# Second-layer V loads between the K loads, three half tiles of K loaded a second time, and softmax denominators on GpSimd, in a two-layer decode kernel

## The chip, the cores and the metric

The kernel runs on one core of a Trainium2 chip. The metric is the device time of one execution in microseconds (us), and the figure compared is the median over several runs. The engines are named as the profile names them: PE is TensorE (PEld its weight loads), DVE is VectorE, ACT is ScalarE, POOL is GpSimd, SP is SyncE, whose queue issues the loads.

## The reference

Four sequences (B = 4) each decode one token with D = 512 channels. Two layers are applied, each an attention block and then a gated feed-forward block, both behind a layer norm and added to the residual. Both layers use **the same weights and the same K and V caches**:

```python
x = x + _A_ref(_layernorm(x), k_cache, v_cache, wq, wo)
x = x + _B_ref(_layernorm(x), w_gate, w_up, w_down)
x = x + _A_ref(_layernorm(x), k_cache, v_cache, wq, wo)   # layer 2: same caches, same weights
x = x + _B_ref(_layernorm(x), w_gate, w_up, w_down)
```

`_A_ref` projects x to 32 query heads of 128; there are 8 groups of K and V, each shared by 4 heads, with 4096 positions: scores, softmax over the positions, weighted sum of V, projection with `wo`. `_B_ref` is sigmoid(x wg) * (x wu), times wd, with F = 1792. All inputs are bfloat16. One group of K or of V of one batch element is 1 MB, so one batch element has 8 MB of K and 8 MB of V.

## The kernel before, in words

**Tiles.** A group of K or V is moved in two half tiles (q = 0, 1) of 128 x 2048 bfloat16, 512 KB each. They go into a ring of 22 slots in SBUF (`ring`, `NS = 22`); all weights have places of their own. In what follows a "load" is one half tile, a "batch" is one of the 4 sequences, written b, and l = 0, 1 is the layer.

**Stages of a batch.** For l = 0 the 16 loads of K are transposed in place by DVE (`transpose_k`, L475), in 32-bit units. `spread` makes a block form of the queries (`q_spread`, a matmul to `M_ps` and a DVE multiply into `qbd`, L466). `scores` (L488) multiplies the queries by the transposed K into one of three PSUM banks `S_ps`, for two halves s of four groups. `softmax` takes the maximum (DVE, L504 to L523), the exponentials with their sums `ls` (ACT, L528), transposes the result on PE through `PT_ps` (L536, L547 copy it out) into `pt_sb`, and makes the inverse denominators `winv`: a DVE product of `ls` and a selector into `dsel` (L553), two fp32 matmuls with ones into `M_ps`, a reciprocal (L559). `values` (L573) multiplies the V loads by `pt_sb` into `O_ps`; a DVE multiply by `winv` takes the result out (L582). `y_proj` applies `wo`. `cross` then does everything from there to the next layer's input: residual, layer norm, wg, wu, the gate, wd, residual, layer norm; `q_proj` makes the queries of layer 1. Matmuls built by the helper `mm` all have line L298.

**Two layers, one load of K.** K of batch b stays in its 16 slots, transposed, until the scores of layer 1 have been made from it; it is loaded once. V is loaded once for each layer: for layer 0 while layer 0's output is formed, and again for layer 1, for which the softmax of layer 1 must be done first.

**Order of the loads.** SP issues all loads in the order in which they are written in the program: wq and K of batch 0, four groups of V, wo, wg, four groups of V, wu, wd; then for b = 1, 2, 3

```python
for g in range(pre):            # pre = 0
    load_v(1, b - 1, g)
load_k(b, 0)
load_k(b, 1)
for g in range(8):
    load_v(0, b, g)
for g in range(pre, 8):
    load_v(1, b - 1, g)
```

and at the end V of batch 3 for layer 1. A load waits until the slot that it gets is free; every load behind it waits too.

**Order of the other work.** A planner (`_Sched.place`) fixes it before the kernel is built. Each piece of work has an engine, an assumed duration and a priority (lower goes first); the planner steps through time and gives every engine a fixed order, and every load a slot, the one that falls free first by its own reckoning. Loads are reckoned at `RATE` GB/us on one shared bus, with constants for the start and the landing. On the chip each engine runs its list strictly in that order and waits at semaphores, so a piece that waits holds up all pieces behind it on its engine. The priorities before are `PX, PS, PV, PC, PK = 0, 2, 2.2, 4, 2.1`: the way through `cross` and `q_proj` first, then layer 1's scores (1), layer 0's (2), the transposes of K (2.1), the V products (2.2).

Of the kernel before, what the change touches and what calls it, by code (L numbers as in the profile page):

```python
# [11 lines left out]
LAT = 0.2  # L12
RATE = 0.409


class _Op:
    __slots__ = (
        "eng", "fns", "dur", "prio", "sem", "inc", "deps", "after", "left", "users", "est", "start", "end", "seq",
        "needed", "value", "tile", "bytes", "lab",
    )  # L20
# [14 lines left out]
class _Sched:  # L35
# [6 lines left out]

    def put(self, eng, fns, dur, prio, reads=(), writes=(), dma=None, tiles=(), uses=(), nbytes=0):
        op = _Op()
        op.eng, op.dur, op.prio, op.bytes = eng, dur, prio, nbytes
        op.fns = list(fns) if isinstance(fns, (list, tuple)) else [fns]
        op.sem, op.inc, op.needed = dma or eng, 16 if dma else 1, dma is not None
        op.value = op.tile = op.start = op.end = None
        op.deps, op.after, op.users = [], [], []
        op.lab = ",".join(list(writes) + [dma or ""])  # L50
        for k in list(reads) + list(writes):
            w = self.last_write.get(k)
            if w is not None:
                self._dep(op, w, eng == "pe" and w.eng == "pe")
        for k in writes:
            for r in self.readers.get(k, ()):
                self._dep(op, r, r.eng == eng and r.sem == eng)
        for t in tiles:
            self._dep(op, t.load, False)
        for t in list(tiles) + list(uses):  # L60
            t.ops.append(op)
        for k in writes:
            self.last_write[k] = op
            self.readers[k] = []
        for k in reads:
            if k not in writes:
                self.readers.setdefault(k, []).append(op)
        op.seq = len(self.all)
        self.all.append(op)
        return op  # L70
# [5 lines left out]
    def load(self, tile, fn, nbytes):  # L76
        op = self.put("sp", fn, 0.55, 0, dma="slot", nbytes=nbytes)
        op.tile = tile
        tile.load = op
        return op  # L80

    def place(self):
# [15 lines left out]
        held = {}  # L98
        spi = 0

        def slot_time(s):
# [16 lines left out]
        while True:  # L118
# [27 lines left out]
            if o.eng == "sp":  # L146
# [11 lines left out]
                if o.bytes:  # L158
                    b0 = max(free_at["bus"], t + o.dur + 1.0)
                    free_at["bus"] = b0 + o.bytes / (RATE * 1e6)  # L160
                    self.bus.append((b0, free_at["bus"], o))
                    finish(o, free_at["bus"] + 1.2)
                else:
                    finish(o, t + 2.5)
            else:
                pending[o.eng].remove(o)
                free_at[o.eng] = t + o.dur
                finish(o, t + o.dur if o.sem == o.eng else t + 2.5)
        left = [o for o in self.all if o.end is None]
# [28 lines left out]
def bass_interleave_layers__gqa_block_cached__glu_gated_glu__decode_kernel(nc, A_x, A_k, A_v, A_wq, A_wo, B_x, B_wg, B_wu, B_wd, out):  # L198
# [67 lines left out]
    winv = [sb(f"winv{i}", [P, 16]) for i in range(4)]  # L266
    dsel = sb("dsel", [P, 2, 16])

# [37 lines left out]
    S.put("sp", lambda e: e.dma_start(x16[0:16, :], A_x.rearrange("b o (k p) -> (b o k) p", k=KD)), 0.55, 0, writes=["x16"], dma="x")  # L306
    S.put("pool", lambda e: e.memset(ident_b[:], 0.0), 0.15, 0, writes=["ident_b"])
    S.put("pool", affine(ident_b, ident_b[:], [[-1, P]], 0, 1.0), 0.3, 0, reads=["ident_b"], writes=["ident_b"])
    for key, ap, v in (("neg", neg, -1.0 / D), ("pos", pos, 1.0 / D), ("mhalf", mhalf, -0.5), ("ones", ones, 1.0)):
        S.put("dve", lambda e, ap=ap, v=v: e.memset(ap, v), 0.08, 0, writes=[key])  # L310
    for name, t in (("mask_a", mask_a), ("sel_den", sel_den)):
        S.put("pool", lambda e, t=t: e.memset(t[:], 0.0), 0.15, 0, writes=[name])
    for g in range(4):
        m = mask_a[32 * g:32 * g + 32, g * R:(g + 1) * R]
        S.put("pool", lambda e, m=m: e.memset(m, 1.0), 0.1, 0, reads=["mask_a"], writes=["mask_a", "sel_den"])
        v = sel_den[:].rearrange("p (g h) -> p g h", g=4)[:, g, :]
        for a in range(4):
            S.put("pool", affine(sel_den, v, [[-1, R]], -(32 * g + 4 * a), 1.0), 0.2, 0, reads=["sel_den"], writes=["sel_den"])
    for name, t, v in (("ml0", ml, 1.0), ("mt", mt, 0.0), ("S0", S_ps[0], 0.0), ("S1", S_ps[1], 0.0), ("S2", S_ps[2], 0.0)):
# [4 lines left out]
    vt = {}  # L324
    K, V = {}, {}

    def load_piece(src, q):
# [8 lines left out]

    def load_k(b, s):
        for q in range(2):
            for g in range(4 * s, 4 * s + 4):
                K[b, g, q] = load_piece(A_k[b, g], q)  # L340

# [4 lines left out]
    def load_w(key, o, i, nbytes):  # L346
        S.put("sp", lambda e: e.dma_start(o, i), 0.55, 0, writes=[key], dma=key, nbytes=nbytes)  # L347

# [28 lines left out]
    load_wd()  # L377
    pre = 0
    for b in range(1, B):
        for g in range(pre):  # L380
            load_v(1, b - 1, g)
        load_k(b, 0)
        load_k(b, 1)
        for g in range(8):
            load_v(0, b, g)
        for g in range(pre, 8):
            load_v(1, b - 1, g)
    for g in range(8):
# [41 lines left out]
    def rstd(mult, rs, rs_key, nb, prio):  # L430
# [6 lines left out]
            "pool", lambda e: e.tensor_tensor(rs, vpe[:, 0:nb], mhalf[:, 0:nb], ALU.pow), 0.6, prio,  # L437
            reads=["vpe", "mhalf"], writes=[rs_key],
        )

    def q_proj(s, xT_of, n, dst, dkey, prio, xkey):
# [9 lines left out]
        S.put("act", lambda e: e.activation(dst, M_ps[:, 0:16 * n], ACTF.Copy), 0.25, prio, reads=["M"], writes=[dkey])  # L451

    cnt = {"u": 0, "o": 0, "pt": 0}

# [14 lines left out]

    def transpose_k(b, g, q, prio):  # L470
        t = K[b, g, q]

        def fn(e):
            v = ring[t.slot].bitcast(dt.int32)
            return e.transpose(v, v)  # L475
        S.put("dve", fn, 1.2, prio, writes=[f"kT{b}{g}{q}"], tiles=[t])

    def scores(b, s, u, prio):
        for q in range(2):
            fns = []  # L480
            bank, bkey = S_ps[(2 * u + q) % 3], f"S{(2 * u + q) % 3}"
            for nn in range(NQ):
                for gi in range(4):
                    t = K[b, 4 * s + gi, q]

# [7 lines left out]
            S.put(  # L493
                "pe", fns, 1.85, prio, reads=[f"qbd{u % NQB}"] + [f"kT{b}{4 * s + gi}{q}" for gi in range(4)],
                writes=[bkey], uses=[K[b, 4 * s + gi, q] for gi in range(4)],
            )

    def softmax(u, rs, rs_key, prio):
# [41 lines left out]
        for t4 in range(4):  # L540
# [8 lines left out]
        )  # L549
        i0 = ls.unsqueeze(2).broadcast_to([P, 2, 16])  # L550
        i1 = sel_den[:].unsqueeze(1).broadcast_to([P, 2, 16])
        S.put(
            "dve", lambda e: e.tensor_tensor(dsel[:], i0, i1, ALU.mult), 0.2, prio + 1,  # L553
            reads=["ls0", "ls1", "sel_den"], writes=["dsel"],
        )
        fns = [mm(M_ps[:, 480:496], col(ones), dsel[:, q, :], q == 0, q == 1) for q in range(2)]
        S.put("pe", fns, 0.7, prio + 1, reads=["dsel", "ones"], writes=["M"])
        S.put(
            "dve", lambda e: e.reciprocal(winv[pi][:], M_ps[:, 480:496]), 0.18, prio + 1, reads=["M"],  # L559
            writes=[f"winv{pi}"],  # L560
# [3 lines left out]
    def values(l, b, s, pi, prio, gis=range(4)):  # L564
        if not len(gis):
            return
        for gi in gis:
# [13 lines left out]
        S.put(  # L581
            "dve", lambda e: e.tensor_tensor(o, O_ps[:, c0:c1], winv[pi][:, c0:c1], ALU.mult), 0.2, prio - 1.5,  # L582
            reads=["O", f"winv{pi}"], writes=[f"oT{l}{s}{gi}" for gi in gis],
# [102 lines left out]

    PX, PS, PV, PC, PK = 0, 2, 2.2, 4, 2.1

# [9 lines left out]
    def attend(l, b, s, prio, u=None):  # L698
        if u is None:
            u = spread(l, b, s, prio)  # L700
        if l == 0:
            for q in range(2):
                for gi in range(4):
                    transpose_k(b, 4 * s + gi, q, PK)
        scores(b, s, u, prio)
        return softmax(u, rs_q[l][:, b:b + 1], "rs_q0" if l == 0 else f"rs_q1{b}", prio)
# [10 lines left out]
    for s in range(NH):  # L717
# [13 lines left out]
        )  # L731
        pis[0, 0, s] = attend(0, 0, s, PS)
    for b in range(B):
        if b > 0:
            values(1, b - 1, 0, pis[1, b - 1, 0], PV, range(pre))
        for s in range(NH):
            for gis in (range(0, 3), range(3, 4)):
                values(0, b, s, pis[0, b, s], PV, gis)
                y_proj(0, s, PX, gis)
        if b > 0:  # L740
            values(1, b - 1, 0, pis[1, b - 1, 0], PV, range(pre, 4))
        cross(0, b, PX)
# [4 lines left out]
        if b < B - 1:  # L747
            us += [spread(0, b + 1, s, PS) for s in range(NH)]
        if b > 0:
            values(1, b - 1, 1, pis[1, b - 1, 1], PV)  # L750
        for s in range(NH):
            pis[1, b, s] = attend(1, b, s, 1, us[s])
        if b < B - 1:
            for s in range(NH):
                pis[0, b + 1, s] = attend(0, b + 1, s, PS, us[NH + s])
    for s in range(NH):
        for gis in (range(0, 3), range(3, 4)):
            values(1, B - 1, s, pis[1, B - 1, s], PV, gis)
            y_proj(1, s, PX, gis)
# [42 lines left out]
```

## Time and profile before

| what | value |
|---|---|
| median of 5 runs | 343.33 us (341.32 to 344.94) |
| the profiled execution: its time, and its span (first to last instruction) | 344.94 us, 342.6 us |
| outside the span in that execution | 2.3 us |
| bytes loaded | 115.32 MB, mean 337 GB/s over the span |
| busy: PE, PEld, DVE, ACT, POOL | 219.7, 170.2, 138.6, 52.6, 10.5 us |
| granted TensorE clock, mean | 0.605 |
| loads: V, K, weights | 128 and 64 of 512 KB; 4 wq and 4 wo of 1 MB; wg, wu, wd of 1.75 MB |

The page's slices show the share of busy time over the span; the row of GB/s shows what the 16 DMA engines moved in each slice. "A <- B" in the table of groups and of waits means that A sat idle until B released it. SPq is the queue that issues the loads.

### The profile page before, as it was taken

What the parts mean: (1) busy time and instruction counts of PE and PEld (TensorE: products, weight loads), DVE (VectorE), ACT (ScalarE), POOL (GpSimd) and SP (SyncE); (2) the same over time, 40 slices, a digit from 0 to 9 for tenths busy, and PEclk for the clock granted to TensorE, in tenths of its full rate; (3) what the DMA queues carried; (4) which work ended last, traced back from release to release, by engine and by line L of the source; (5) the groups of instructions that cost most, each with busy time, mean ns of one, the idle gap of its engine ahead of it and who ended that gap; (6) DMA issues with size and microseconds to landing.
All of it is one profiled execution on the core that took longest, in us unless ns stands there. A gap on an engine that the chain in (4) does not pass through costs nothing.

```text
span 342.6 us, 11870 instructions
## 1 busy us (share of the span) xinstructions
PE 219.7 (64%) x5426; PEld 170.2 (50%) x5426; DVE 138.6 (40%) x338; ACT 52.6 (15%) x128; POOL 10.5 (3%) x38
## 2 busy tenths in 40 slices
PE   1332861264678694878843896789546968796666
PEld 1202551154634283776521485784324758765566
DVE  3777620000859820101599730015998300143011
ACT  1003030000023330000322130002312300014000
POOL 6000000000000000000000000000000000000001
PEclk9999965555565555555855555557655555578555
DMA  7999999999559979978899999979999999989910
GB/s 264 379 397 408 409 349 366 409 404 374 204 158 397 401 239 411 383 276 309 267 407 408 371 353 362 371 273 322 388 412 408 378 326 416 318 291 367 409 77 2
DMA packets 36897, 115.32 MB, mean 337 GB/s; under 512 B 3312, under 2 KB 9200, under 8 KB 36848
## 3 DMA queue, kind: packets, MB, share of 16 engines
q1 hardware_dynamic: 36816, 114.57, 89.3%
q8 instruction: 42, 0.69, 0.8%
q14 instruction: 7, 0.06, 0.0%
q10 hardware_dynamic: 32, 0.00, 0.0%
HBM read 114.56 MB, written 0.00 MB: 334 GB/s over the span
## 4 chain that ended last, share of the span: by engine, by line
DMA 42%; PE 29%; DVE 14%; SPq 7%; issue 6%; ACT 1%; DVEq 0%; ACTq 0%
DMA ring<-in_A_v_cache_dram 30%; DMA ring<-in_A_k_cache_dram 10%; PE O_ps L573 7%; PE S_ps L488 6%; PE Y_ps L298 6%; DVE ring L475 6%; SPq L331 5%; PE M_ps L298 4%; PE G_ps L298 3%; DMA wo<-in_A_wo_dram 3%; DVE ml L504 3%; SPq L347 2%; PE PT_ps L298 1%; ACT p_sb L528 1%; DVE qbd L466 1%
## 5 line engine op out<-in xcount | busy, mean ns | idle before, releaser
L573 PE MATMUL O_ps<-pt_sb,ring 128*128 128x4 bf16 x2048 | 67.5, 166 | 41.4 <-DMA ring<-in_A_v_cache_dram 30.3
L573 PEld LDWEIGHTS O_ps<-pt_sb,ring 128*128 128x128 bf16 x2048 | 62.8, 104 | 49.8 <-issue 24.3
L475 DVE STREAM_TRANSPOSE ring<-ring 128x1024 int32<-128x1024 int32 x64 | 76.7, 1223 | 14.8 <-DMA ring<-in_A_k_cache_dram 14.6
L488 PE MATMUL S_ps<-ring,qbd 128*16 128x512 bf16 x512 | 53.3, 567 | 13.1 <-DVE ring L475 13.1
L528 ACT ACTIVATE p_sb<-S_ps,cols 128x512 bf16<-128x512 f32 x32 | 24.6, 772 | 85.5 <-DVE cols L523 85.5
L582 DVE TENSOR_TENSOR oT<-O_ps,winv 128x12 bf16<-128x12 f32 (+2 forms) x26 | 4.5, 174 | 79.0 <-PE O_ps L573 78.9
L504 DVE TENSOR_REDUCE ml<-S_ps 128x1 f32<-128x512 f32 x32 | 21.6, 674 | 33.5 <-PE S_ps L488 33.5
L488 PEld LDWEIGHTS S_ps<-ring,qbd 128*16 128x16 bf16 x512 | 13.2, 108 | 34.6 <-issue 16.2
L298 PE MATMUL Y_ps<-oT,wo 128*128 128x1 bf16 (+1 forms) x640 | 20.4, 166 | 8.3 <-DVE oT L582 5.0
L298 PEld LDWEIGHTS Y_ps<-oT,wo 128*128 128x128 bf16 x640 | 18.9, 105 | 10.3 <-DVE oT L582 6.2
L298 PE MATMUL M_ps<-dsel,cols 128*128 128x16 f32 x64 | 15.9, 368 | 12.0 <-DVE qbd L466 9.2
L298 PE MATMUL PT_ps<-ident_b,p_sb 128*128 128x64 bf16 x128 | 11.0, 229 | 15.7 <-ACT p_sb L528 15.6
L298 PEld LDWEIGHTS M_ps<-dsel,cols 128*128 128x128 f32 x64 | 14.6, 316 | 12.5 <-DVE qbd L466 9.4
L298 PEld LDWEIGHTS PT_ps<-ident_b,p_sb 128*128 128x128 bf16 x128 | 7.6, 120 | 24.6 <-ACT p_sb L528 21.6
L298 PE MATMUL M_ps<-xT,wq 128*128 128x1 bf16 x512 | 15.0, 165 | 3.4 <-DVE qbd L466 1.5
L437 POOL TENSOR_TENSOR cols<-cols 128x1 f32<-128x1 f32 (+1 forms) x10 | 6.4, 638 | 322.8 <-issue 211.7
L426 ACT ACTIVATE gs<-xj,cols 128x4 f32<-128x4 f32 x8 | 2.4, 298 | 90.4 <-DVE cols L424 90.4
L298 PEld LDWEIGHTS M_ps<-xT,wq 128*128 128x128 bf16 x512 | 14.3, 104 | 3.7 <-DVE qbd L466 1.6
L298 PE MATMUL G_ps<-cols 128*128 128x1 f32 (+1 forms) x40 | 11.4, 354 | 3.0 <-DVE xj L664 1.0
L547 ACT ACTIVATE pt_sb<-PT_ps 128x512 bf16<-128x512 f32 x16 | 9.5, 596 | 21.5 <-PE PT_ps L298 21.5
L536 ACT ACTIVATE p_sb<-PT_ps 128x512 bf16<-128x512 f32 x16 | 9.6, 597 | 15.6 <-PE PT_ps L298 15.6
L298 PE MATMUL PT_ps<-p_sb,ident_b 128*32 128x128 bf16 x256 | 9.6, 289 | 3.4 <-issue 2.7
(73 smaller groups left out, 146.0 us busy)
## 6 DMA issues: line engine op xcount, KB each, us to landing
ring<-in_A_v_cache_dram SPq DMA_DIRECT2D x128, 512.0 KB, 7.8
ring<-in_A_k_cache_dram SPq DMA_DIRECT2D x64, 512.0 KB, 11.1
wq<-in_A_wq_dram SPq DMA_DIRECT2D x4, 1024.0 KB, 12.5
wo<-in_A_wo_dram SPq DMA_DIRECT2D x4, 1024.0 KB, 11.2
wg<-in_B_w_gate_dram SPq DMA_DIRECT2D x1, 1792.0 KB, 13.3
wu<-in_B_w_up_dram SPq DMA_DIRECT2D x1, 1792.0 KB, 12.7
wd<-in_B_w_down_dram SPq DMA_DIRECT2D x1, 1792.0 KB, 17.5
x<-in_A_x_dram SPq DMA_DIRECT2D x1, 4.0 KB, 1.5
```

What stands on the lines that cost most here:

```text
L298: return lambda e: e.matmul(o, lhsT=l, rhs=r, start=start, stop=stop)
L331: return e.dma_start(ring[t.slot], t.src.rearrange("(p t) d -> p (t d)", p=P)[:, q * TS:(q + 1) * TS])
L347: S.put("sp", lambda e: e.dma_start(o, i), 0.55, 0, writes=[key], dma=key, nbytes=nbytes)
L437: "pool", lambda e: e.tensor_tensor(rs, vpe[:, 0:nb], mhalf[:, 0:nb], ALU.pow), 0.6, prio,
L475: return e.transpose(v, v)
L488: return e.matmul(bank[32 * gi:32 * gi + 16, :], lhsT=qbd[u % NQB][:, gi, nn, :], rhs=kt[:, :, nn // 2, :, nn % 2], start=nn == 0, stop=nn ...
L504: "dve", lambda e, q=q: e.tensor_reduce(ml[:, q:q + 1], S_ps[banks[q]][:], AX.X, ALU.max, negate=True), 0.65,
L528: "act", lambda e, q=q: e.activation(p_sb[:, 4 * q:4 * q + 4, :].rearrange("p c x -> p (c x)"), S_ps[banks[q]][:], ACTF.Exp, bias=nbias, s ...
L536: "act", lambda e: e.activation(pt1.rearrange("p c g a h -> p (c g a h)"), PT_ps[:], ACTF.Copy), 0.65, prio,
L547: "act", lambda e: e.activation(pt_sb[pi][:].rearrange("p q c g h -> p (q c g h)"), PT_ps[:], ACTF.Copy), 0.65,
L573: return e.matmul(O_ps[:, gi * R:(gi + 1) * R], lhsT=ring[tile.slot][:, (t % HT) * DH:(t % HT + 1) * DH], rhs=pt_sb[pi][:, t % 4, t // 4, ...
L582: "dve", lambda e: e.tensor_tensor(o, O_ps[:, c0:c1], winv[pi][:, c0:c1], ALU.mult), 0.2, prio - 1.5,
```

## The change

The change has five parts.

1. **Order of the loads.** The order for each of b = 1, 2, 3 is a string: `k` is two half tiles of K(b), `v` one group (two loads) of V for layer 1 of batch b - 1, `V` one group of V for layer 0 of batch b, `r` the second loading of K.
2. **Three half tiles of K a second time.** The loads (group 6, q = 1), (7, 0) and (7, 1) of each batch are no longer kept from layer 0 to layer 1; their slots fall free after layer 0's scores, and they are loaded and transposed again for layer 1 (`reload_k`). The other 13 are kept as before. For batch 0 the second loading stands behind wd.
3. **Denominators.** On POOL, the two columns of `ls` are added, and one product with the selector makes a `dsel` of 16 columns; one fp32 matmul takes the place of two.
4. **The V products** of the groups loaded early stand in the program ahead of those of layer 0, the rest where they stood.
5. **The planner's constants and priorities.**

```diff
-RATE = 0.409
+RATE = 0.4165
+START = 2.3
+LAND = 0.5
+RAMP = 0.3
...
-                    b0 = max(free_at["bus"], t + o.dur + 1.0)
-                    free_at["bus"] = b0 + o.bytes / (RATE * 1e6)
+                    b0 = max(free_at["bus"], t + START)
+                    ramp = 3 if b0 > free_at["bus"] else max(ramp - 1, 0)
+                    free_at["bus"] = b0 + o.bytes / (o.rate * 1e6) + (RAMP if ramp else 0.0)
                     self.bus.append((b0, free_at["bus"], o))
-                    finish(o, free_at["bus"] + 1.2)
+                    finish(o, free_at["bus"] + LAND)
...
+    again = ((6, 1), (7, 0), (7, 1))
...
+    def load_k(b, s, qs=(0, 1), gis=range(4)):
+        for q in qs:
+            for g in gis:
+                g += 4 * s
+                K[0, b, g, q] = load_piece(A_k[b, g], q)
+                if (g, q) not in again:
+                    K[1, b, g, q] = K[0, b, g, q]
+
+    def reload_k(b):
+        for g, q in again:
+            K[1, b, g, q] = load_piece(A_k[b, g], q)
...
+    order_b = ['kkkvkkkvkkVVVVVVVVvvvvvvr', 'kkkvkkkvkkVVVVVVVVvvvvvvr', 'kkkvkkkkvkVVVVVVVVvvvvvvr']
+    pres = [o.split("V")[0].count("v") for o in order_b]
+    reload_k(0)
...
-        i0 = ls.unsqueeze(2).broadcast_to([P, 2, 16])
-        i1 = sel_den[:].unsqueeze(1).broadcast_to([P, 2, 16])
-        S.put(
-            "dve", lambda e: e.tensor_tensor(dsel[:], i0, i1, ALU.mult), 0.2, prio + 1,
-            reads=["ls0", "ls1", "sel_den"], writes=["dsel"],
-        )
-        fns = [mm(M_ps[:, 480:496], col(ones), dsel[:, q, :], q == 0, q == 1) for q in range(2)]
-        S.put("pe", fns, 0.7, prio + 1, reads=["dsel", "ones"], writes=["M"])
+        pd = prio + PDEN
+        S.put(
+            "pool", lambda e: e.tensor_tensor(ls[:, 0:1], ls[:, 0:1], ls[:, 1:2], ALU.add), 0.6, pd, reads=["ls0", "ls1"],
+            writes=["ls0", "pl"],
+        )
+        S.put(
+            "pool", lambda e: e.tensor_scalar(dsel[:], sel_den[:], ls[:, 0:1], None, op0=ALU.mult), 0.6, pd,
+            reads=["ls0", "sel_den"], writes=["dsel", "pl"],
+        )
+        S.put("pe", mm(M_ps[:, 480:496], col(ones), dsel[:]), 0.6, pd, reads=["dsel", "ones"], writes=["M"])
...
-    PX, PS, PV, PC, PK = 0, 2, 2.2, 4, 2.1
+    PX = 0
+    PS0, PS1, PL0, PL1, PV0, PV1, PK0, PK1, PDEN, PEV = (2, 0.42, 1, 1, 1.15, 1.7, 2.1, 2.1, 1.1, 1.6)
...
+        else:
+            for g, q in again:
+                if g // 4 == s:
+                    transpose_k(1, b, g, q, (PL0, PL1)[s])
```

In the priorities, PS0 and PS1 are layer 0's scores and softmax for s = 0 and 1, PL0 and PL1 layer 1's, PV0 and PV1 the V products of the layers, PK0 and PK1 the transposes, PDEN is added for the denominators, PEV is the multiply by `winv`. A new key `pl`, written by every POOL instruction, makes each of them wait for the one before it.

## The prediction

> **What bounds the kernel now.** I read the sliced page first, then the waits of SP's queue, then the windows of the stages.
>
> ```profile
> PE 219.7 (64%) x5426; PEld 170.2 (50%) x5426; DVE 138.6 (40%) x338; ACT 52.6 (15%) x128; POOL 10.5 (3%) x38
> ...
> DMA  7999999999559979978899999979999999989910
> GB/s 264 379 397 408 409 349 366 409 404 374 204 158 397 401 239 411 383 276 309 267 407 408 371 353 362 371 273 322 388 412 408 378 326 416 318 291 367 409 77 2
> ```
>
> No engine is busy two thirds of the time, and DMA is near 9 in most slices. But the GB/s row falls from 410 to 158-330 again and again: loading bounds the kernel, with holes. The waits of SP's queue, where the issue of loads itself stands still (total us, times, longest):
>
> ```profile
> SPq L331 <- PE O_ps L573: 76.0, 58, 5.5
> ...
> SPq L190 <- PE S_ps L488: 26.4, 5, 15.4
> ```
>
> L331 is the issue of a ring load. It waits for a slot that the V products hold, and once for 15.4 us for slots that the scores of layer 1 hold. Windows over one whole period (busy us of PE, PEld, DVE, ACT, POOL; clock; DMA share; GB/s):
>
> ```profile
> 211.90:233.60 21.70, 18.40 (x540) 16.51 (x544) 2.27 (x15) 1.42 (x7) 1.08 (x2) 0.50 0.88 323
> 233.60:259.20 25.60, 15.77 (x287) 8.87 (x290) 23.12 (x45) 7.74 (x17) 0.00 (x0) 0.63 1.01 389
> 259.20:281.55 22.35, 17.12 (x432) 13.77 (x424) 7.68 (x19) 3.55 (x8) 0.00 (x0) 0.50 1.00 365
> ```
>
> The first stretch is the cross stage of batch 2: PE busy 18.4 of 21.7, DVE idle, 323 GB/s. The second is the K stage: DVE busy 23.1 of 25.6, PE light, 389 GB/s. The third forms layer 0's output. So the holes lie where PE is full, not where DVE is.
>
> **The price of a load.** In an undisturbed stretch loads land 1.275 us apart: by the trace's landing times, 18 of them from 172.58 to 195.54 us (22.96/18). I cut the run by landings:
>
> - wd lands at 85.31. Until then the DMA engines have few holes.
> - 160 ring loads follow; the last lands at 329.41. 244.1 us, less 160 x 1.275 = 204.0, leaves **40.1 us of holes**.
> - Tail from 329.41 to the end of the span: 13.2 us. 85.3 + 204.0 + 40.1 + 13.2 = 342.6.
>
> By stage, with T(b) the landing of the last V load of layer 0 of batch b (139.36, 211.93, 281.55): wd to T(1) 13.2, T(1) to T(2) 11.4, T(2) to T(3) 8.4, T(3) to the last landing 7.1. The largest single hole is behind wd: six loads of K(1) land until 92.86, and the next at 101.48, 7.35 us more than a load takes. The slots are freed by layer 1's scores of batch 0, which start at 95.11 at the end of the chain from wd:
>
> ```profile
> 90.00:95.00 5.00, 3.50 (x125) 3.39 (x123) 4.40 (x6) 0.18 (x1) 0.55 (x1) 0.50 0.10 35
> 95.00:100.00 5.00, 5.00 (x87) 1.99 (x84) 2.08 (x5) 0.18 (x1) 0.00 (x0) 0.56 0.35 97
> ```
>
> **The change part by part.**
>
> *Second loading of K.* 4 x 3 = 12 more loads; at 1.275 us that is **+15.3 us** of DMA time. Here a rule speaks against the change. The Trainium skill, "SBUF — State Buffer", section "The DMA setup-cost knee", gives each transfer some 2 us of fixed cost beside its bytes at 436 GB/s: 2 + 1.2 = 3.2 us a load, 38.4 us for twelve, and then the change loses (about 358 us in the sum below). The row decides otherwise: queued loads land 1.275 us apart; the fixed part shows only as delay (3.5 to 18.2 us from issue to landing). I take 15.3.
>
> The three loads of batch 0 stand between wd and K(1). They land at 86.6 to 89.2, the six K loads until 96.8, while the first slots still come free at 97.07. Three loads of the 7.35 us hole are filled: **3.4 us** of it stays, at no cost to that stage.
>
> *DVE.* 12 more transposes of 1.223 us (L475): +14.7 us in all, 3.7 per batch; away go 16 L553 of 0.15, -2.4. They are due at the end of the cross stage, where DVE is busy 2.27 of 21.70. That hides them. Without the cover they cost up to 3.7 us per batch, since layer 1's scores of s = 1 wait for them, and DVE's short layer-norm and `qbd` steps (0.15 to 0.42 us) stand in the same list behind them.
>
> *Three more free slots.* From layer 0's scores to the second loading, V has 9 slots instead of 6: 9 x 1.275 = 11.5 us of loads in flight instead of 7.7. Issue to landing takes 3.5 to 4.7 us where the queue has run dry. So a slot could be held 3 to 4 us without a hole, and now 7 to 8. In the cross stages SP stood between two issues for 3.8, 4.3, 2.5, 5.0 us (batch 1) and 4.9, 3.1, 2.7, 3.6 (batch 2), while PE did wd, `q_proj` and layer norm first. These are above the old bound and below the new.
>
> *V of layer 1 between the K loads.* 4 of the 16 loads leave the cross stage. Their products (16 matmuls, about 0.43 us each load by the spacing of the rows) go with them: 1.7 us off the stage where PE is full, into the K stage, where DVE sets the pace and K need only arrive at DVE's speed. Does the cross stage still have loads enough? From T(b): 12 + 3 + 6 of the next K = 21 x 1.275 = 26.8 us; layer 1's scores free the first slots about 21.7 us behind T (233.62 - 211.93), and 4.5 us later a load lands: 26.2. Just enough. Before: 22 loads, 28.1. By then PE had consumed 10 of the 16 V loads; if it is 10 of 12 now, two slots fail, 1 to 2 us of hole per batch.
>
> *Denominators.* PE: 4 fp32 passes, 1.01 us, become 2, 0.5 us: 8 us over 16 softmaxes, some on the full stage, the rest beside DVE. POOL gains 32 instructions; the nearest row is L437, 0.54 us for one column and 1.03 for four, so I take 0.55 for the add and 0.3 to 1.0 for the product. `winv` comes some 0.5 us earlier or later and is wanted several us after; at 198.75 it was late (the reciprocal just ahead of the `oT` multiply at 199.04), because `dsel` stood behind transposes on DVE. POOL is idle, so this wait can shrink by 1 us. POOL's own list also holds the rstd step of the cross stage; it would stand behind a denominator only if that waited for exponentials there. Bounds -1 to +1 us per batch; I take 0. A POOL instruction beside a transpose (93.00, 0.55 us; transpose at 93.18, 1.23 us) did not lengthen it.
>
> *Planner constants.* They alter orders, not durations. I can't read their gain from this trace: bounded by the holes themselves (between none and all), and below by a worse order, some us. It is in the share below.
>
> **Sum.** Without the hole behind wd, 40.1 - 7.35 = 32.8 us of holes. They come in shallow queues; in the long queued stretches (245.12 to 274.41, 23 loads, 1.273 each) there are none, so deeper queues should close them. The ends are none left and all left. I take 40% left: 9 slots cover the single holds, while 26.8 against 26.2 us leaves a remainder at each gate. Loss: 3.4 + 13.1 = 16.5. Span: 85.3 + 172 x 1.275 (219.3) + 16.5 + 13.2 = **334.3**, against 342.6 in its own execution: -8.3 us, with the 2.3 us outside it 336.6 against 344.94. On the median of 343.33 that is **335 us**. Break-even: 40.1 - 15.3 - 3.4 = 21.4 us, 65% of the 32.8, left.
>
> **Rivals.** About 1% is what a measurement of this kernel tells from no change.
>
> 1. *The holes close almost wholly* (15% left): loss 8.3, span 326.1, **327 us**. For it: the K stage shows that loads can run without holes for 30 us. Against it: the gate at layer 1's scores has 0.6 us to spare. Chance 0.18.
> 2. *The trade is even*: the second loading takes its three slots back just before layer 1's scores, so at the gate nothing is gained; 60 to 70% of the holes stay: **343 us**. For it: 21 loads of cover against 22. Chance 0.16.
> 3. *Slower: the second loading arrives late.* It is last in the line of the batch, so each wait for a slot ahead of it delays it, then three transposes, then the scores of s = 1, and with them the next K. The place is DVE's list ahead of layer 1's scores. It decides once the three loads land later than the scores of s = 0 (21.7 us behind T; without holes they land at 15 x 1.275 = 19.1). Then all 32.8 us of holes stay, beside 15.3 of loads: span 354.0, **355 us**; half-way 348. Before, DVE stood behind K in this way (a transpose group 89.22 to 92.88 ahead of the `qbd` step). Chance 0.23.
>
> **How the numbers follow.** Forecast 335 us at 0.43. Faster by over 1% (below 339.9): 0.43 + 0.18 = 0.61. Within 1%: 0.16. Slower: 0.23. The range runs from 325 (the first rival with a little less) to 351 (well into the third).
>
> **What would show it.** K loads 76 rather than 64 (V 128 as before), 6.3 MB more, and a mean above 355 GB/s (121.6 MB over 334 us is 364). SP's wait for O_ps at L331 well below 76 us. The wait for S_ps of 15.4 us near 11. L475 x76. `M_ps<-dsel` matmuls 32 instead of 64. The period between the last V loads of layer 0, 72.6 and 69.6 us before, near 69. Wrong would be a new DVE wait on the K loads in the cross stage, or scores at L488 waiting long for DVE.

## The result, and the profile after

| | before | after |
|---|---|---|
| median | 342.45 us (80 runs) | 338.48 us (43 runs) |
| profiled execution: time, span | 344.94, 342.6 us | 338.28, 336.5 us |
| ratio to before | 1 | **0.9898**, 95% interval 0.9881 to 0.9914 |

The change makes the kernel 1.0% faster, 4.0 us; forecast were 335 us, 8.3 us less. The profiled execution of before was a slow one, 2.5 us above its median.

The page after: busy times, DMA share and GB/s by slice, and q8, a queue of instruction packets.

```profile
PE 215.2 (64%) x5394; PEld 165.9 (49%) x5394; DVE 149.5 (44%) x337; ACT 52.5 (16%) x128; POOL 19.2 (6%) x70
...
DMA  7999999999959999999899999998999999999910
GB/s 264 379 402 410 408 369 363 409 406 369 405 196 381 412 408 406 406 410 376 298 370 411 411 404 409 409 354 323 329 414 411 408 408 406 392 328 329 414 52 2
...
q8 instruction: 42, 0.69, 0.8%
```

The GB/s row has long runs of 404 to 412 where before had 270 to 380. What is left stands in four places, each one to three slices wide (196; 298; 323 and 329; 328 and 329): behind wd, and once in each later batch. SP's waits after (total us, times, longest) say the same:

```profile
SPq L337 <- PE O_ps L599: 64.9, 55, 5.3
SPq L337 <- PE M_ps L303: 34.0, 8, 14.3
...
SPq L195 <- PE S_ps L510: 23.7, 8, 8.6
```

L337 is the issue of a ring load. The wait for V products (`O_ps`) fell only from 76.0 to 64.9. The stand behind wd, which before was the 15.4 us for layer 1's scores, is not the 8.6 (that one lies in the first 50 us): it is the 14.3 us put down to `M_ps`, whose matmuls stand in PE's list right behind those scores. So it is hardly shorter. A wait alone costs nothing: with nine loads queued SP may stand still longer. So I read the stages (busy us of PE, PEld, DVE, ACT, POOL; clock; DMA share; GB/s), cut at the last V load of layer 0 and at the first slot that layer 1's scores free:

```profile
209.55:233.90 24.35, 19.04 (x577) 17.21 (x577) 7.97 (x19) 1.42 (x7) 1.12 (x2) 0.50 0.95 365
233.90:258.30 24.40, 15.09 (x280) 7.94 (x268) 21.59 (x43) 7.87 (x17) 1.57 (x6) 0.64 1.00 379
258.30:279.40 21.10, 15.55 (x410) 12.58 (x403) 6.09 (x16) 3.42 (x7) 0.52 (x2) 0.50 1.03 408
```

The V stage is full: 408 GB/s against 365. The cross stage of batch 2 moves 365 instead of 323 but **lasts 24.35 us where it lasted 21.70**. The account by landings, as in the prediction:

| | wd lands | holes wd to T(1) | T(1) to T(2) | T(2) to T(3) | to the last landing | all holes | tail | span |
|---|---|---|---|---|---|---|---|---|
| before | 85.31 | 13.2 | 11.4 | 8.4 | 7.1 | 40.1 | 13.2 | 342.6 |
| after | 83.53 | 5.9 | 5.4 | 4.8 | 5.2 | 21.4 | 12.3 | 336.5 |

"Holes" is the time between two landings less 1.275 us a load. After has 172 ring loads from wd on, so 219.3 us at 1.275; 83.5 + 219.3 + 21.4 + 12.3 = 336.5. Holes of 18.7 us are closed, 15.3 us of loads are added.

### The profile page after: what moved, and what is told of

Its sections match the earlier page's. It is cut to its first block, busy times and chain, and to the rows that moved or that the text cites. A ratio compares the mean times of both kernels' runs of the same rounds, so it can differ in the third digit from the quotient of the medians.

```text
span 336.5 us, 11884 instructions
## 1 busy us (share of the span) xinstructions
PE 215.2 (64%) x5394; PEld 165.9 (49%) x5394; DVE 149.5 (44%) x337; ACT 52.5 (16%) x128; POOL 19.2 (6%) x70
## 4 chain that ended last, share of the span: by engine, by line
DMA 45%; PE 26%; DVE 12%; SPq 12%; issue 4%; ACT 1%; DVEq 0%; ACTq 0%
DMA ring<-in_A_v_cache_dram 22%; DMA ring<-in_A_k_cache_dram 17%; PE O_ps L599 6%; SPq L337 6%; PE Y_ps L303 6%; DVE ring L497 6%; DMA wu<-in_B_w_up_dram 5%; SPq L361 5%; PE S_ps L510 5%; PE M_ps L303 4%; PE G_ps L303 3%; DVE ml L528 2%; PE PT_ps L303 2%; ACT p_sb L552 1%; DVE qbd L488 1%
## 5 line engine op out<-in xcount | busy, mean ns | idle before, releaser
L599 PE MATMUL O_ps<-pt_sb,ring 128*128 128x4 bf16 x2048 | 68.8, 166 | 53.7 <-DMA ring<-in_A_v_cache_dram 38.4
L497 DVE STREAM_TRANSPOSE ring<-ring 128x1024 int32<-128x1024 int32 x76 | 90.9, 1222 | 24.2 <-DMA ring<-in_A_k_cache_dram 23.9
L608 DVE TENSOR_TENSOR oT<-O_ps,winv 128x12 bf16<-128x12 f32 (+3 forms) x29 | 5.0, 171 | 87.6 <-PE O_ps L599 87.6
L552 ACT ACTIVATE p_sb<-S_ps,cols 128x512 bf16<-128x512 f32 x32 | 24.6, 772 | 78.0 <-DVE cols L547 63.9
L510 PEld LDWEIGHTS S_ps<-ring,qbd 128*16 128x16 bf16 x512 | 14.1, 106 | 32.8 <-issue 14.7
L528 DVE TENSOR_REDUCE ml<-S_ps 128x1 f32<-128x512 f32 x32 | 21.6, 674 | 16.5 <-PE S_ps L510 16.5
L303 PE MATMUL Y_ps<-oT,wo 128*128 128x1 bf16 (+1 forms) x640 | 20.4, 166 | 7.8 <-DVE oT L608 4.1
L303 PEld LDWEIGHTS Y_ps<-oT,wo 128*128 128x128 bf16 x640 | 18.7, 104 | 10.0 <-DVE oT L608 5.3
L303 PE MATMUL PT_ps<-ident_b,p_sb 128*128 128x64 bf16 x128 | 11.3, 232 | 13.1 <-ACT p_sb L552 13.0
L303 PE MATMUL M_ps<-xT,wq 128*128 128x1 bf16 x512 | 15.4, 165 | 5.1 <-issue 2.6
L303 PEld LDWEIGHTS PT_ps<-ident_b,p_sb 128*128 128x128 bf16 x128 | 7.2, 117 | 19.0 <-ACT p_sb L552 15.2
L303 PE MATMUL G_ps<-cols 128*128 128x1 f32 (+1 forms) x40 | 11.4, 354 | 3.0 <-DVE xj L690 1.0
L576 POOL TENSOR_TENSOR cols<-cols 128x1 f32<-128x1 f32 x16 | 3.1, 194 | 159.8 <-ACT p_sb L552 159.8
L303 PEld LDWEIGHTS G_ps<-cols 128*128 128x128 f32 x40 | 10.0, 311 | 3.4 <-DVE cols L424 1.2
L303 PE MATMUL Y_ps<-hT,wd 128*128 128x1 bf16 (+1 forms) x280 | 8.4, 166 | 5.3 <-DMA wd<-in_B_w_down_dram 2.7
## 6 DMA issues: line engine op xcount, KB each, us to landing
wq<-in_A_wq_dram SPq DMA_DIRECT2D x4, 1024.0 KB, 12.3
wu<-in_B_w_up_dram SPq DMA_DIRECT2D x1, 1792.0 KB, 18.5
```

Of the source, the lines that this page charges most:

```text
L303: return lambda e: e.matmul(o, lhsT=l, rhs=r, start=start, stop=stop)
L510: return e.matmul(bank[32 * gi:32 * gi + 16, :], lhsT=qbd[u % NQB][:, gi, nn, :], rhs=kt[:, :, nn // 2, :, nn % 2], start=nn == 0, stop=nn ...
L528: "dve", lambda e, q=q: e.tensor_reduce(ml[:, q:q + 1], S_ps[banks[q]][:], AX.X, ALU.max, negate=True), 0.65,
L552: "act", lambda e, q=q: e.activation(p_sb[:, 4 * q:4 * q + 4, :].rearrange("p c x -> p (c x)"), S_ps[banks[q]][:], ACTF.Exp, bias=nbias, s ...
L599: return e.matmul(O_ps[:, gi * R:(gi + 1) * R], lhsT=ring[tile.slot][:, (t % HT) * DH:(t % HT + 1) * DH], rhs=pt_sb[pi][:, t % 4, t // 4, ...
```

## The experiments

Ratios are to the kernel before on the same chip, in brackets the 95% interval. "Gate" is the time from T(b) to the first matmul of layer 1's scores; "issue gaps" are PE's waits of over 0.7 us in it that no semaphore explains (`<-issue`).

### First: each part undone or alone

```diff
-    again = ((6, 1), (7, 0), (7, 1))
+    again = ()
```

> As after, but all 16 half tiles of K are kept from layer 0 to layer 1: no second loading, 6 slots for V. Theory A (the three slots close the holes and are worth more than the 15.3 us of loads): slower than after, 342 to 350 us, with SP's wait for O_ps back near 76 us. Theory B (the order of V, the planner's constants and the denominators close the holes; the second loading only about pays for itself): 335 to 341 us, within 1% of after. Theory C (the second loading costs more than it brings): below 335 us.

340.86 us, 0.9965 (0.9933 to 0.9996). SP's waits without the second loading:

```profile
SPq L337 <- PE O_ps L599: 72.3, 62, 5.2
...
SPq L195 <- PE S_ps L510: 30.9, 5, 15.4
```

The stand behind wd is 15.4 us (14.3 in after), and the holes are 36.6 us in its profile. So the second loading closes 36.6 - 21.4 = 15.2 us of holes for 15.3 us of loads: in the profiles that is a draw, and the 2.0 us between the spans lie in the start (1.1) and the tail (1.0). In the medians it is worth 2.4 us. The time is in theory B's range, and B was right that the balance is small; but not the order, the constants and the denominators close the holes (36.6 are left without the second loading, 40.1 before), it is the second loading with its slots, as A had it.

The denominators back as they were (DVE product of both columns, two fp32 matmuls), the rest as after:

```diff
-        S.put("pool", lambda e: e.tensor_tensor(ls[:, 0:1], ls[:, 0:1], ls[:, 1:2], ALU.add), ...
-        S.put("pool", lambda e: e.tensor_scalar(dsel[:], sel_den[:], ls[:, 0:1], None, op0=ALU.mult), ...
+        S.put("dve", lambda e: e.tensor_tensor(dsel[:], i0, i1, ALU.mult), 0.2, prio + 1, ...
```

> As after, but the denominators as before: the product on DVE, two fp32 matmuls. Theory A (off the path, cost zero): within 0.3% of after, 337.5 to 339.5 us. Theory B (PE relieved by 0.5 us per softmax on the way to the first free slots): 2 to 8 us slower than after.

344.25 us, 1.0047 (1.0011 to 1.0083): 5.8 us slower than after. I had them at nothing.

```diff
-    order_b = ['kkkvkkkvkkVVVVVVVVvvvvvvr', 'kkkvkkkvkkVVVVVVVVvvvvvvr', 'kkkvkkkkvkVVVVVVVVvvvvvvr']
+    order_b = ['kkkkkkkkVVVVVVVVvvvvvvvvr'] * 3
```

> As after, but no V of layer 1 stands between the K loads: K, V of layer 0, all V of layer 1, then the second loading. Theory A (in the cross stage 16 V loads with 9 slots cover the chain as well as 12 do; DVE is fed early): within 1% of after. Theory B (the four loads moved out of the cross stage relieve PE by 1.7 us per batch, and give the K stage its pace): 342 to 347 us.

343.72 us, 1.0046 (1.0012 to 1.0079): theory B by its time. With the order goes the V products' place (part 4), so the two are not told apart. The second loading without the new order is slower than before; holes 29.2 us. But the gates are as long as in after (22.1 us in the mean in both), so it is not in the gate that PE is relieved.

The planner's constants and priorities alone (without PDEN, which belongs to the new denominators), on the orders and engines of before:

> As before (K kept, V behind K, denominators on DVE), with the planner's new constants and priorities alone. Theory A (they alter orders only by chance): 341 to 345 us, no difference from before that can be measured. Theory B (they are much of the gain): 337 to 340 us. One write after a read of the small maximum tile waits at a semaphore in addition; that costs nothing by either.

342.19 us, 1.001 (0.9973 to 1.0047): theory A, nothing. Its holes are 40.2 us, those of before 40.1; wd lands at 83.41, and the tail is 12.1 us.

### Second: slots without loads, denominators, and a shift of PE's program

```diff
-    NS = 22
+    NS = 25
-    wu = sb("wu", [P, KD, F], bf)
+    wu = wg
```

> Second loading off (all K kept), and 25 ring slots instead of 22: the place comes from wu, which is loaded into the place of wg (same bytes, but the gate and the up product are both made from wu). So V has 9 slots all the time and no load is added. Theory A (slots close the holes, each load costs 1.275 us): holes like those of after (about 21 us instead of 36.6), hence 15 us below the kernel without second loading, 325 to 328 us. Theory B (the gate at layer 1's scores keeps the holes whatever the slots): 334 to 339 us.

338.69 us, 0.9887 (0.9857 to 0.9916). Theory B, and the clearest miss of the first theory: three more slots for no loads at all were to give 15 us, and give 2.2 beside the kernel without second loading.

```profile
SPq L337 <- PE O_ps L599: 89.2, 57, 10.7
...
SPq L195 <- PE S_ps L510: 28.8, 4, 15.8
```

The holes only fell from 36.6 to 30.3, the wait for layer 1's scores behind wd stayed at 15.8, and the tail grew from 13.3 to 18.6. In the gates, 25.7, 27.5 and 22.8 us, PE is busy 18.0, 18.3 and 17.7 us and stands 6.2, 7.4 and 3.4 in issue gaps: **PE sets the pace** there, not the slots.

The denominators' two steps on DVE, still one matmul:

> As after, but the add and the product of the denominators on DVE instead of GpSimd; still one fp32 matmul. Theory A (DVE's list is what GpSimd relieves): as slow as with the old denominators, 342 to 345 us. Theory B (PE relieved of one fp32 matmul each): as after, 337.5 to 340 us. Theory C (PE's instruction fetch decides, and falls differently in each program): anything from 336 to 345 us, following the sum of PE's issue gaps ahead of layer 1's scores (11.2 us in after, 16.5 with the old denominators).

342.43 us, 0.999 (0.9963 to 1.0017): theory A by its time. But theory C is not excluded: its gates have 17.2 us of issue gaps, 6.0 more than after. PE's and DVE's orders are rearranged by the planner as well, so more than the place of two steps differs.

The gates of these runs have up to 17.2 us of PE's issue gaps, after has 11.2. So the program on PE was shifted and nothing else:

```diff
+    S.put("pe", [mm(G_ps[:, 400:401], ident_b[:], ident_b[:, 0:1]) for _ in range(64)], 0.0, PX, reads=["ident_b"], writes=["pad"])
```

> As after, with 64 small matmuls (128 by 1, into an unused PSUM column) put first on PE, where it idles until the first input lands; every engine's order is otherwise that of after. It moves the place in PE's instruction stream at which each fetch falls. Theory F (PE's instruction fetch stands on the way to the gate): the time changes by 2 us or more in either direction, and the change is that of PE's issue gaps. Theory N (it does not): within 0.3% of after, 337.5 to 339.5 us.

> As the last, with 32 of the small matmuls. Theory F: another time than after and than with 64, by the issue gaps. Theory N: within 0.3% of after.

337.47 us, 0.9855 (0.9833 to 0.9878) with 64, and 339.45, 0.9919 (0.989 to 0.9947) with 32. The intervals of the two don't meet: they are 2.0 us apart. But each differs from after by only 1.0 us, half of what theory F asked for and at the edges of theory N's range, so neither is shown. In the three gates the gaps add up to 11.7 us (64), 14.9 (32) and 11.2 (after): the slower of the two shifts has more, while after with the fewest stands between.

### Third: what makes the gaps

SP holds a load back until the sixth before it has landed:

```diff
+        ring_loads = [o for o in order["sp"] if o.tile is not None]
+        for o, d in zip(ring_loads[24 + 6:], ring_loads[24:]):
+            o.deps.append(d)
```

> As after, orders and slots unchanged, but SP issues a ring load only when the sixth load before it has landed, so at most 6 loads are queued instead of up to 9 and more. Theory D (the deep queue itself holds up PE's instruction fetch: PE's issue gaps ahead of layer 1's scores were 2.5 us a stage with 6 slots and 4.8 with 9): gaps fall to some 2.5 us a stage, and the time to 334 to 337 us. Theory S (it is the share of time in which the DMA engines are busy, not the depth): gaps as in after, time 337.5 to 340 us. If 6 are too few to bridge the delay from issue to landing: 342 us or more, with new holes in the V stages.

337.7 us, 0.9845 (0.9814 to 0.9876). The gaps in the gates are 5.1, 4.0 and 2.6 us, against 5.3, 3.3 and 2.6: theory D falls, the depth of the queue is not their cause. Six loads in flight are enough (holes 21.2 us, in after 21.4).

```diff
-            V[l, b, g, q] = load_piece(A_v[b, g], q)
+        V[l, b, g, 0] = V[l, b, g, 1] = load_piece(A_v[b, g], 0)
```

> As after, but each group of V is loaded as one half tile, which is used for both halves: 64 V loads less (33.5 MB), the same instructions on PE, DVE and ACT. So the DMA engines have pauses. Theory F (PE's instruction fetch waits because the DMA engines are full with loads): PE's issue gaps, 13.2 us in all in after, fall to 3 us or less, and the way from the last V product of layer 0 to layer 1's scores to about 18 us. Theory G (the fetch itself is too slow for PE's pace, whatever else moves): gaps stay at 10 us or more. Time by either 270 to 300 us.

308.53 us, above the range I gave. GB/s falls to 131 to 215 in the gates' slices (88 MB are loaded instead of 122), and the gaps remain, 12.3 us in all against 13.2. PE rows around one, from its timeline (start, us, what, idle before):

```profile
127.33 1.15 PE L598 MATMUL O_ps<-pt_sb,ring 128*128 128x4 bf16 x38
...
132.89 0.41 PE L598 MATMUL O_ps<-pt_sb,ring 128*128 128x4 bf16 x10 [4.41 <-issue]
```

PE stops for 4.4 us amid a row of equal matmuls whose tile it has already begun. Theory G: DMA engines full with loads are not needed for the gaps. Since the V loads here run ahead of the plan, the gates' lengths (29 to 31 us) can't be compared with the others.

The kernel before, with the 64 matmuls first:

> The kernel before, with 64 small matmuls put first on PE, orders unchanged. Theory F: the time of before depends on where the fetches fall as well, 340 to 345 us, so that 1 to 2 us of the difference between before and after are the luck of this place. Theory N: within 0.3% of before.

344.78 us, 1.0052 (1.0018 to 1.0085): slower if anything, in the range of theory F, though the interval reaches into theory N's 0.3%.

The kernel with the old denominators (e2 in the expectation) and the same 64 matmuls:

> As e2 (denominators on DVE, two matmuls), with the 64 small matmuls first on PE. Theory L (the 5.8 us by which e2 was slower than after are where its fetches fall): back to 337 to 340.5 us. Theory G (GpSimd's product and the fp32 matmul saved are worth several us by themselves): 342 us or more.

343.25 us, 1.0009 (0.9978 to 1.004), where after with the same shift takes 337.47. Theory G by its time: the 5 to 6 us stay with the denominators within this plan at a second place of the fetches. By which way is open: the gates of the three kernels with denominators on DVE have 16.5 (two matmuls), 18.5 (the same, shifted) and 17.2 us (one matmul) of issue gaps, those of after and its shift 11.2 and 11.7, so the gaps may be the way and are not ruled out.

### Fourth: what was still open

The denominators' change alone, on the kernel before:

> The kernel before, with only the denominators changed (add and product on GpSimd, one fp32 matmul). Theory P (the denominators are worth 4 to 6 us wherever they stand, as in the runs with the rest of the change): 337 to 339.5 us. Theory I (they pay only together with the V loads between the K loads, whose products stand on PE behind the denominators' matmul): within 1% of before, 340 to 345 us. One more wait of a write after a read, on winv, costs nothing by either.

**347.0 us, 1.0144 (1.01 to 1.0187)**: slower by 4.6 us. Neither theory. Nearly the same edit (one priority and one wait differ) costs 1.4% here and is worth 1.5% there (0.9898 against 1.0047), and its holes are 45.3 us instead of 40.1. So it has no fixed price of its own; that the planner's whole order around it moves is the likely reason, not a shown one. Its gates have 11.2 us of issue gaps against 6.8 in before. Which step decides was not settled.

```diff
-'kkkvkkkvkkVVVVVVVVvvvvvvr'
+'kkkvkkkvkkVVVVVVVVvvvvrvv'
```

> As after, but for b = 1 to 3 the second loading of K stands ahead of the last two groups of V instead of behind them, so that its three transposes fall earlier on DVE, not between the layer-norm and qbd steps ahead of layer 1's scores. Theory R (those transposes hold up the gate: qbd stood 0.8 us behind one at 157.3): gate 1 us shorter per batch, 335 to 337.5 us. Theory S (the slots given back earlier cost the V stream as much): 338 to 342 us.

339.94 us, 0.993 (0.9897 to 0.9964): theory S. The gates grew to 23.4, 25.4 and 24.6 us; less their gaps (5.2, 6.7, 5.9) they are 18.2, 18.7 and 18.6, as in after (18.3, 19.1, 17.6). So the place of these transposes does not set the gate. After's own trace, in batch 1, says why:

```profile
158.13 0.39 DVE L488 TENSOR_TENSOR qbd<-M_ps,mask_a 128x256 bf16<-128x256 f32 x1
...
161.02 1.84 PE L303 MATMUL M_ps<-xT,wq 128*128 128x1 bf16 x64
...
162.80 1.89 PE L510 MATMUL S_ps<-ring,qbd 128*16 128x512 bf16 x16
```

`qbd` is ready at 158.52 and the first score runs at 162.80; until 160.30 PE stands in an issue gap, and then come 27 V products and 64 `wq` matmuls. In the two later gates PE's weight loads wait for `qbd` for 0.2 us each.

> As after, with at most 6 loads queued and the 64 small matmuls first on PE together; each alone gave 337.5 to 337.7 us. If both gains are real and independent: 336 to 337 us. If they are the luck of where the fetches fall: 337 to 339.5 us.

338.34 us, 0.9869 (0.983 to 0.9909). The two gains don't add. Each alone ends just below after's interval (0.9878 and 0.9876 against 0.9881), the two together do not, so no gain over after is established.

> As the kernel without second loading, with the 64 small matmuls first on PE. If the 2.3 us between it (340.86) and after are those of the second loading and not of the fetches' place: 340 to 342.5 us, against 337.5 for after with the same 64. If they are the place: 338.5 us or less.

341.35 us, 0.9957 (0.9926 to 0.9988), against 0.9855 for after with the same shift. With 0.9965 against 0.9898 unshifted, the second loading is worth 0.7 to 1.0% at both places of the fetches, not the 15 us net that theory A of the 25 slots gave its slots.

### The gates of all kernels

Each PE gap is preceded by one packet of 16 KB on queue q8, and PE resumes 2.2 to 2.7 us after that packet's start: all 31 gaps in the traces of before, after, half V and the shift by 64. 42 such packets are 0.69 MB, the page's line for q8; with 64 more matmuls and their weight loads there are 43, which fits a queue for PE's instructions. Two stretches of PE's timeline, before and after, in the same stage of batch 1 (layer 0's sum is done, layer 1's queries are made):

```profile
150.96 0.59 PE L298 MATMUL Y_ps<-hT,wd 128*128 128x1 bf16 x16 [2.19 <-issue]
...
160.04 0.30 PE L298 MATMUL M_ps<-xT,wq 128*128 128x1 bf16 x6 [1.25 <-issue]
```

```profile
149.03 0.51 PE L599 MATMUL O_ps<-pt_sb,ring 128*128 128x4 bf16 x13 [1.92 <-issue]
...
154.16 1.66 PE L303 MATMUL M_ps<-xT,wq 128*128 128x1 bf16 x56 [1.08 <-issue]
...
160.30 0.86 PE L599 MATMUL O_ps<-pt_sb,ring 128*128 128x4 bf16 x27 [2.34 <-issue]
```

Before loses 3.4 us in two stops, after 5.3 in three. Each breaks off in the middle of a group that PE had begun. Over the gates of all kernels that make full loads (before and its shift are left out of the first row; with them it is 20.6, 2.9 and 17.7):

| | gates | gate, mean | issue gaps in it | rest |
|---|---|---|---|---|
| V has 6 slots (4 kernels) | 12 | 20.4 us | 2.8 us | 17.6 us |
| V has 9 slots (11 kernels) | 33 | 23.2 us | 4.9 us | 18.3 us |
| before | 3 | 20.2 us | 2.3 us | 17.9 us |
| after without the second loading | 3 | 21.1 us | 3.8 us | 17.3 us |
| after | 3 | 22.1 us | 3.7 us | 18.4 us |

In the mean of these kernels the rest is nearly one number. With 9 slots the gate is 2.8 us longer, 2.1 of it issue gaps, and 11 to 14 V loads are worked off in it where it was 9 to 11. That PE, no longer stopped by missing V loads, runs into its own instruction supply fits this; no run shows that it is the reason. The pair that differs in the second loading alone does not have it: the gaps are 3.8 and 3.7 us a gate, and after's gate is 1.0 us longer because PE is busy longer (16.9 us against 16.1), with 12.3 V loads worked off instead of 11.2. With 64 matmuls ahead, the same pair has gaps of 2.0 and 3.9. Nor do the gaps alone set the time: 25 slots have 17.0 us of them in three gates at 338.69 us, the denominators on DVE 16.5 at 344.25.

## Why the prediction was wrong, point by point

**The sum.** Span forecast 334.3, measured 336.5. The terms:

- *Time to wd and tail*: taken as unchanged, 85.3 and 13.2; measured 83.5 and 12.3. 2.7 us in the change's favour that had no step.
- *A load at 1.275 us*: right, also for the second loading. From 181.50 to 224.80 us 34 loads land 1.274 us apart. The estimate of 3.2 us from the knee, weighed against it, would have been far off for queued loads.
- *The hole behind wd*: forecast 3.4 left; the load behind it lands 3.0 late, but the next two land 1.7 and 1.0 late as well, so this hole is 5.7, not 3.4.
- *The other holes*: forecast 13.1 left (40% of 32.8), measured 21.4 - 5.9 = 15.5. **The step that failed is "layer 1's scores free the first slots about 21.7 us behind T" and "4.5 us later a load lands: 26.2. Just enough"**, carried over from before, where the three batches had 22.9, 21.7 and 21.9. In after the first load into such a slot was issued 25.6, 24.4 and 22.1 us behind T and landed at 31.8, 30.1 and 28.1, against 26.8 us of cover.

Where the holes behind T(1) lie (us):

| | ahead of the load into that slot | this load and the next seven | later |
|---|---|---|---|
| before | 13.8 | 8.7 | 4.3 |
| after without the second loading | 15.5 | 7.1 | 4.9 |
| after | 6.4 | 8.0 | 1.1 |
| 25 slots, no second loading | 8.0 | 8.9 | 1.4 |

So the slots did more than halve the holes of the single holds, as forecast, but at the gate nothing was gained. The slot comes late because PE's list takes longer to reach those scores (23.7, 22.4 and 20.1 us, before 20.9, 19.7 and 19.9): in the three gates together PE is busy 1.7 us more, with more V products ahead of the scores, and stands 4.4 us more in issue gaps. The granted clock is 0.50 in the cross stage before and after, so it is not the difference. Why the gaps are longer stays open. The 6.4 us are left because the holds do not come one by one: between 143.65 and 164.73 SP stood 5.9, 1.9, 1.4, 3.4, 2.9 and 3.5 us between two issues, and the prediction held each alone against 7 to 8 (two of the eight that it lists, 2.5 and 2.7, were not above the old bound either). The third gate's slot came nearly as forecast, and still 5.2 us of holes stand there; only 19 loads lay ahead of it, not 21.

So the holes came out 4.9 us larger and start and tail 2.7 smaller: 2.2 us on the span.

**The base.** 334.3 plus the time outside the span is 336.6 for a profiled execution; after's took 338.28. That this is off by only 1.7 us is luck: the 4.9 us of holes are set against 2.7 us of start and tail and 0.5 outside the span. Start and tail are not the change's: wd lands between 83.3 and 84.7 in the other kernels with full loads, with and without the change's parts. The planner-only kernel, which has before's loads and no measured difference in time, has wd at 83.41, 40.2 us of holes and a tail of 12.1. Against it the change closes 18.8 us of holes for 15.3 us of loads, 3.5 us, and the medians of before and after are 4.0 apart. The forecast had 23.6 for 15.3, 8.3 us. So the miss is in the holes. The 343.33 us from which the 8.3 were taken were 0.9 above the median of 80 runs; that hid a part of it.

**The parts.** *Planner constants*: no effect, as held possible. *Slots*: worth their loads and little more: the change breaks even at 40.1 - 15.3 = 24.8 us of holes, and 21.4 were left. *V between K*: the runs gave it 5.2 us (343.72 to 338.48), which is 1.7 us for each of three batches, but not by a shorter gate. *Denominators*: forecast 0 with bounds of 1 us per batch; within the change they are worth 5.8 us and alone they cost 4.6. The bounds priced the instructions; the order of all engines moves with them, which the bounds left out. The parts do not add: 5.8, 5.2 and 2.4 us for taking out each of three, and 4.0 for all. The instructions themselves were cheaper than taken, the add 0.19 us and the product

```profile
L580 POOL TENSOR_SCALAR dsel<-sel_den,cols x16: 326/326/337, 27.6 to 312.6; 128x16 f32<-128x16 f32 x16
```

0.33 us. *DVE*: as forecast,

```profile
L497 DVE STREAM_TRANSPOSE ring<-ring 128x1024 int32<-128x1024 int32 x76 | 90.9, 1222 | 24.2 <-DMA ring<-in_A_k_cache_dram 23.9
```

76 transposes of 1.222 us, not lengthened by POOL beside them.

**The rivals and the signs.** The second was right that at the gate nothing is gained, but the slots taken back are not the reason: with 25 slots none is taken back, and 8.9 us stand there all the same. Its 343 us did not come. The third (the second loading's transposes hold up layer 1's scores) was right in place, not in cause: the gate is late, but PE waits for `qbd` 0.2 us at most, and placing those loads earlier did not shorten it. Of the signs, 76 K loads, 361 GB/s and periods of 70.4 and 69.9 us came, and the stand behind wd did not fall to 11 (14.3). The sign of being wrong, a DVE wait for K loads in the cross stage, came too: 3.0, 2.7 and 2.3 us in the three gates, none in before. By the 0.2 us above it is not what holds up PE.

## What to carry to other kernels

Holes in the load stream at a gate are closed by slots only as far as the chain that frees them stays as long as it was; look at what stands ahead of that chain's first step in its engine's list, here V products, projections and stops at instruction packets. Waits that follow one another must be added up against the cover, not held against it one by one. A forecast of an absolute time can come near by errors that cancel; check it term by term, with a second kernel of the same loads where there is one. Where a planner fixes all orders, the price of one edit measured in one setting (here -1.5% and +1.4%) says nothing of it in another.

## What the runs showed of the hardware that was not expected

The 16 KB packets on q8 fit PE's instructions, and in those four traces PE stands 0.8 to 2.7 us (once 4.4) at some of them in stages of many small matmuls, 13.2 us in all in after. The Trainium skill, "Runtime: NRT & Kernel Launch", section "Instruction fetch mechanics", calls the crossing of a 16 KB block mostly hidden; in after that holds for 35 of the 42 packets, and 7 are followed by a stop, six of them in the gates. Neither a shallower load queue (14.8 us of such gaps) nor 28% less traffic (12.3) took them away. Moving the boundaries by 32 or 64 matmuls gave medians of 339.45 and 337.47 us, where after has 338.48. That PE waits for the packet is read from the times alone; no run took the packets away.
